# The clamp of phi's exponential moved from VectorE to GpSimd, in a kernel with a sliding-window and a linear attention block

## The chip, the cores and the metric

One core of a Trainium2 chip. The metric is the device time of one execution in microseconds (us). The kernel before was run three times: 291.31 us median, 289.54 to 292.64. Engine names as in the profile: PE is TensorE (PEld its weight loads), DVE is VectorE, ACT is ScalarE, POOL is GpSimd, SP is SyncE.

## What is computed

Two independent attention blocks, A and B, whose outputs stand side by side in the result. Each has an input x of 2048 tokens by 640, a weight wqkv of 640 by 1920 and wo of 640 by 640, in bf16, and 32 heads of 20. A is softmax attention over a window of 256 tokens. B is linear attention, and phi belongs to it:

```
phi = lambda t: jnp.where(t > 0, t + 1, jnp.exp(t)) + 1e-6
pq, pk = phi(q), phi(k)
kv = einsum("bhsd,bhse->bhde", pk, v);  z = einsum("bhsd->bhd", pk)
o = einsum("bhqd,bhde->bhqe", pq, kv) / (einsum("bhqd,bhd->bhq", pq, z)[..., None] + 1e-6)
```

The kernel writes phi(t) as max(t, 0) + min(exp(t) + 1e-6, 1 + 1e-6): for t > 0 the second part is the constant 1 + 1e-6, for t <= 0 the first part is 0. "The clamp" is the second part without the exponential (add, then minimum); "the sum" is the maximum with 0 and the addition.

## The kernel before

**Tiling.** Tokens are taken in 4 blocks (s = 0 to 3) of 512 (SB), and in tiles of 128. The 640 columns are 5 chunks of 128 (KT). A projection is a chain of 5 matmuls (L194) that accumulate in one PSUM bank, named "dense". There are three such banks (`dps`, 3 buffers); S_ps takes four banks, O_ps one.

**Two streams on PE.** The main stream is block A's attention, in 90 units. `scores` (L474) computes the scores of a unit into S_ps (L483), lets ACT make p from them with one exponential of 128x2048 (L491), and lets GpSimd cut p to the window with one or two selects (L505). `values` (L516) multiplies p with the values (L527) and, at the end of a group, normalises on DVE (L549, L550). `values` of a unit is issued after `scores` of the unit two later (LAG = 2). Into this stream a second one, `fill`, is woven: all projections, block B, and the output projections. After each unit `take` (L657) draws as many matmul columns from `fill` as the unit is due, an equal share.

**Queues.** The schedule is manual: each engine executes its instructions in the order in which the program issues them, and waits on semaphores for the other engines.

**phi.** `phi` (L200) is called at the end of a chain, with the bank as `src`. It issues the exponential on ACT at once (L203, into a tile e with 4 buffers). The clamp (L207) and the sum (L210) are put on the list `later`, and `flush` issues them: after the next cast that frees a bank (`evac`, L181), or after the exponential of the next phi, whichever is first. Both run on DVE. The sum is the last reader of the bank.

**Stages with phi.** Each of the eight stages calls phi five times, 40 in all:

- `b_kv(s)` (L355), four times: rows of k by the chains of `tok_rows`, in turn with the chains of the values (cast on DVE into vB), then the products of k and v (L377), added up in kv_acc and at last kv_bd (L385, L388). At the start GpSimd fills the ones in vB (L358); in `b_kv(3)` GpSimd cuts kv_bd to the own head with ten selects (L163).
- `b_q(s)` (L410), four times: phi of q. `b_q(0)` runs in turn with A's projections for block 3, `b_q(1)` alone, `b_q(2)` and `b_q(3)` in turn with output projections. `b_num` (L425) then reads phi of q (L436) and divides on DVE (L445 to L449).

In the order of time: b_kv(0) at about 41 to 61 us, b_kv(1) at 62 to 81, b_kv(2) at 81 to 100, b_kv(3) at 126 to 146, b_q(0) at 146 to 161, b_q(1) at 186 to 198, b_q(2) at 212 to 228, b_q(3) at 241 to 258.

**Other work in GpSimd's queue.** Three weight loads that it issues after the first unit's scores (L106, L617), the ones in vA (L309), and seven output DMAs of the output projections (L349), each of which waits for the last cast into its tile.

Of the kernel before, what the change touches and what calls it, by code (L numbers as in the profile page):

```python
# [10 lines left out]
ALU = mybir.AluOpType  # L11
# [41 lines left out]
def kernel(  # L53
# [10 lines left out]
    nc = tc.nc  # L64
# [10 lines left out]
    def pool(name, bufs, space=None):  # L75
        if space is None:
            return ctx.enter_context(tc.tile_pool(name=name, bufs=bufs))
        return ctx.enter_context(tc.tile_pool(name=name, bufs=bufs, space=space))
# [10 lines left out]
    op1 = pool("o1", 2)  # L89
# [86 lines left out]
    def flush():  # L176

        while later:
            later.pop(0)()
# [20 lines left out]
    def phi(dst, src, view=lambda t: t[:]):  # L200

        e = sp.tile([P, SB], BF16, name="e")
        nc.scalar.activation(out=view(e), in_=src, func=ACT.Exp)  # L203
        flush()

        def rest():
            nc.vector.tensor_scalar(  # L207
                out=e[:], in0=e[:], scalar1=1e-6, scalar2=1.0 + 1e-6, op0=ALU.add, op1=ALU.min
            )
            nc.vector.scalar_tensor_tensor(  # L210
                out=dst, in0=src, scalar=0.0, in1=view(e), op0=ALU.max, op1=ALU.add
            )

        later.append(rest)
# [140 lines left out]
    def b_kv(s):  # L355
# [4 lines left out]
        def done(tb, ps):  # L360
            if tb is None:
                phi(pk[:, :, SB:D], ps, lambda t: t[:].rearrange("p (t n) -> p t n", n=P))
            else:
                phi(pk[:, tb, 0:SB], ps[:])
# [45 lines left out]
    def b_q(s):  # L410
        xt = xB[NS + s]
        pq = pqp.tile([P, KT, SB], BF16, name="phi")
        pq_of[s] = pq
        for c in range(KT):
            ps = bank()
            yield from chain(
                ps[:],
                lambda kt: w_sb["B"][:, kt, c * P : (c + 1) * P],
                lambda kt: xt[:, kt, :],
                SB,  # L420
            )
            phi(pq[:, c, :], ps[:])
            yield End(SB)
# [292 lines left out]
```

## Time and profile before

| What | Value |
|---|---|
| Runs of the kernel before | 291.31 us median, 289.54 to 292.64 |
| The profiled execution | 290.37 us, span 288.5 us |
| Granted TensorE clock in it | 1.00 |
| L203, exponential of phi, ACT, 128x512 | 40 of 591 to 628 ns |
| L207, clamp, DVE, 128x512 bf16 | 40 of 282 to 1409 ns, median 373 |
| L210, sum, DVE, 128x512 | 40 of 691 to 694 ns |
| L491, exponential of the scores, ACT, 128x2048 | 90, mean 1878 ns |
| L505, selects of p, POOL | 178, 145.1 us; of 512 columns 120, mean 690 ns; of 1024 columns 56, mean 1114 ns |
| DMA, mean rate | 124 GB/s |

The profile is one execution on the chip. Busy time is the time in which an engine executes an instruction of the program. The chain is followed back from the last instruction: at each step to what released it, or to the instruction before it on its engine. In a line of a group, the numbers after the first bar are busy us and mean ns of one; after the second bar stand the idle time of the engine just before these instructions, and what ended it. In a line of the timeline, the first number is the start in us, the second the duration; xN means that N neighbours are merged, and in brackets stands the idle time before, and its releaser. "dense", "e", "p", "phi" are tiles of the kernel.

### The profile page before, as it was taken

How to read it: one execution, taken by the hardware profiler on the slowest of the kernel's cores; microseconds unless marked ns; L12 is line 12 of the kernel's file. 1: busy time of each engine (PE TensorE's matmuls, PEld its weight loads, DVE VectorE, ACT ScalarE, POOL GpSimd, SP SyncE). 2: the span in 40 equal slices, each digit the busy share in tenths (PEclk: the TensorE clock that was granted, in tenths of full speed). 3: DMA queues.
4: the chain of work that ended last, by engine and by line, in shares of the span. 5: the costliest groups of instructions: out<-in, count | busy, mean ns of one | idle time of the engine just before them, and what ended most of it. 6: DMA issues, size and time to landing. Idle time of an engine off the chain costs nothing.

```text
span 288.5 us, 8169 instructions
## 1 busy us (share of the span) xinstructions
PE 273.9 (95%) x3512; PEld 159.1 (55%) x3512; DVE 183.5 (64%) x409; ACT 193.4 (67%) x137; POOL 161.0 (56%) x212
## 2 busy tenths in 40 slices
PE   7999999999999999999999899998999999998995
PEld 7644555665666644565654554444545464545653
DVE  0666646847855744556657884458866887677861
ACT  2000058978889777789888767797688878976402
POOL 2000039657576666776699556666665766665620
PEclk9999999999999999999999999999999999999999
DMA  7997699999173172362062543079755145022486
GB/s 245 291 320 197 166 197 251 269 107 207 36 118 70 24 69 93 94 138 46 2 128 59 113 49 114 4 179 151 129 113 72 70 70 137 2 93 48 130 168 204
DMA packets 66676, 35.91 MB, mean 124 GB/s; under 512 B 50801, under 2 KB 65265, under 8 KB 66641
## 3 DMA queue, kind: packets, MB, share of 16 engines
q1 hardware_dynamic: 63792, 27.04, 49.5%
q0 software_dynamic: 1536, 7.05, 7.7%
q10 hardware_dynamic: 1312, 1.31, 1.4%
q8 instruction: 27, 0.44, 0.6%
q14 instruction: 9, 0.07, 0.1%
HBM read 12.45 MB, written 10.49 MB: 79 GB/s over the span
## 4 chain that ended last, share of the span: by engine, by line
PE 58%; ACT 17%; DVE 9%; issue 6%; DMA 6%; POOL 2%; SPq 0%; ACTq 0%; POOLq 0%
PE dense L194 35%; ACT p L491 14%; PE S_ps L483 10%; PE O_ps L527 9%; DMA k_scr<-st 2%; ACT e L203 2%; DMA kpad<-k_scr 2%; DVE phi L210 2%; PE dense L377 2%; DMA oT<-otokA 2%; PE dense L146 2%; DVE e L207 1%; POOL p L505 1%; DVE osb L185 1%; DVE otokB L449 1%
## 5 line engine op out<-in xcount | busy, mean ns | idle before, releaser
L491 ACT ACTIVATE p<-S_ps 128x2048 bf16<-128x2048 f32 x90 | 169.0, 1878 | 72.9 <-PE S_ps L483 68.2
L505 POOL TENSOR_SCALAR_AFFINE_SELECT p<-p 128x512 bf16<-128x512 bf16 (+2 forms) x178 | 145.1, 838 | 112.3 <-ACT p L491 112.2
L527 PEld LDWEIGHTS <-p 128*128 128x128 bf16 x1440 | 42.4, 96 | 19.7 <-issue 16.2
L527 PE MATMUL O_ps<-vA,p 128*128 128x21 bf16 x1440 | 51.1, 173 | 0.8 <-POOL p L505 0.7
L194 PE MATMUL dense<-wB,xB 128*128 128x320 bf16 (+2 forms) x320 | 49.3, 298 | 0.2 <-DVE phi L210 0.2
L194 PE MATMUL dense<-xA,wA 128*128 128x512 bf16 x200 | 46.1, 379 | 0.0
L185 DVE CAST st<-dense 128x512 bf16<-128x512 f32 x40 | 27.4, 690 | 20.5 <-PE dense L194 18.7
L483 PE MATMUL S_ps<-qpad,kpad 20*128 20x256 bf16 (+2 forms) x736 | 36.1, 269 | 2.9 <-ACT p L491 0.5
L185 DVE CAST osb<-dense 128x512 bf16<-128x512 f32 (+1 forms) x39 | 25.2, 647 | 16.1 <-PE dense L194 16.0
L194 PEld LDWEIGHTS <-xA 128*128 128x128 bf16 x320 | 26.4, 97 | 15.6 <-issue 1.5
L194 PEld LDWEIGHTS <-xB 128*128 128x128 bf16 x320 | 26.1, 97 | 13.3 <-issue 1.2
L483 PEld LDWEIGHTS <-kpad 20*128 20x128 bf16 x736 | 15.0, 92 | 32.4 <-issue 29.2
L194 PEld LDWEIGHTS <-wA 128*128 128x128 bf16 x200 | 18.5, 97 | 19.6
L210 DVE SCALAR_TENSOR_TENSOR phi<-dense,e 128x512 bf16<-128x512 f32 x40 | 27.7, 692 | 1.4
L194 PE MATMUL dense<-woA,oT 128*128 128x512 bf16 (+1 forms) x160 | 25.8, 299 | 2.7 <-DVE osb L185 1.6
L207 DVE TENSOR_SCALAR e<-e 128x512 bf16<-128x512 bf16 x40 | 21.2, 530 | 11.2 <-ACT e L203 11.1
L194 PE MATMUL dense<-xB,wB 128*128 128x512 bf16 x100 | 25.7, 378 | 0.9 <-DVE phi L210 0.8
L194 PE MATMUL dense<-wA,xA 128*128 128x320 bf16 x160 | 24.9, 299 | 1.4 <-DVE otokB L449 0.8
L194 PE MATMUL dense<-woB,xA 128*128 128x512 bf16 (+1 forms) x160 | 25.3, 299 | 0.5 <-PE dense L436 0.4
L203 ACT ACTIVATE e<-dense 128x512 bf16<-128x512 f32 x40 | 23.4, 593 | 0.2 <-PE dense L194 0.2
L185 DVE CAST vB<-dense 128x320 bf16<-128x320 f32 x32 | 15.2, 488 | 11.5 <-PE dense L194 11.1
L549 DVE RECIPROCAL recA<-O_ps 128x16 f32<-128x16 f32 (+1 forms) x34 | 8.5, 250 | 20.8 <-PE O_ps L527 20.7
(35 smaller groups left out, 152.0 us busy)
## 6 DMA issues: line engine op xcount, KB each, us to landing
out_dram<-osb POOLq DMA_DIRECT2D x7, 640.0 KB, 3.9
qpad<-q_scr SPq DMA_DIRECT2D x16, 160.0 KB
kpad<-k_scr SPq DMA_DIRECT2D x16, 160.0 KB
wA<-in_A_wqkv_dram SPq DMA_DIRECT2D x3, 800.0 KB
q_scr<-st SPq DMA_DIRECT2D x3, 640.0 KB
k_scr<-st SPq DMA_DIRECT2D x3, 640.0 KB
wB<-in_B_wqkv_dram SPq DMA_DIRECT2D x2, 800.0 KB
wB<-in_B_wqkv_dram POOLq DMA_DIRECT2D x1, 800.0 KB, 10.8
```

Of the source, the lines that this page charges most:

```text
L146: nc.tensor.matmul(ps[:, 0:P], lhsT=ident[:], rhs=ident[:], start=True, stop=True)
L185: nc.vector.tensor_copy(out=dst, in_=src)
L194: nc.tensor.matmul(dst, lhsT=lhs(kt), rhs=rhs(kt), start=(kt == 0), stop=(kt == KT - 1))
L203: nc.scalar.activation(out=view(e), in_=src, func=ACT.Exp)
L207: nc.vector.tensor_scalar(out=e[:], in0=e[:], scalar1=1e-6, scalar2=1.0 + 1e-6, op0=ALU.add, op1=ALU.min)
L210: nc.vector.scalar_tensor_tensor(out=dst, in0=src, scalar=0.0, in1=view(e), op0=ALU.max, op1=ALU.add)
L377: nc.tensor.matmul(pv, lhsT=pk[:, tb, c * P : (c + 1) * P], rhs=vB[:, tb, a : b + 1, :], start=(tb == 0), stop=(tb == TPS - 1),)
L483: nc.tensor.matmul(S_ps[:, j, blk * P : blk * P + n], lhsT=kt[32 * j : 32 * j + DH, g, ko : ko + P], rhs=q_pad[s][32 * j : 32 * j + DH, g, ...
L491: nc.scalar.activation(out=p[:], in_=S_ps[:], func=ACT.Exp, scale=scale)
L505: nc.gpsimd.affine_select(out=v, in_=v, pattern=[[0, 4], [0, b1 - b0], [sgn, P]], compare_op=ALU.is_ge, fill=0.0, base=0 if kind == "D" el ...
L527: nc.tensor.matmul(O_ps[:, slot, j, :], lhsT=p[:, j, b * P : (b + 1) * P], rhs=v_tok[kb // TPS][:, kb % TPS, 4 * gg + j, :], start=(first ...
L549: nc.vector.reciprocal(out=r[:, 0:n, :, :], in_=O_ps[:, :, :, DH:HV])
```

## The change

The clamp is issued on GpSimd instead of DVE, and at the call of phi, behind the exponential, instead of at the flush. Its operands are the same: e from SBUF to SBUF, in place. The sum stays on DVE and is issued at the flush as before.

```diff
         e = sp.tile([P, SB], BF16, name="e")
         nc.scalar.activation(out=view(e), in_=src, func=ACT.Exp)
+        nc.gpsimd.tensor_scalar(
+            out=e[:], in0=e[:], scalar1=1e-6, scalar2=1.0 + 1e-6, op0=ALU.add, op1=ALU.min
+        )
         flush()
 
         def rest():
-            nc.vector.tensor_scalar(
-                out=e[:], in0=e[:], scalar1=1e-6, scalar2=1.0 + 1e-6, op0=ALU.add, op1=ALU.min
-            )
             nc.vector.scalar_tensor_tensor(
                 out=dst, in0=src, scalar=0.0, in1=view(e), op0=ALU.max, op1=ALU.add
             )
```

## Prediction

> **What bounds the kernel now.** I read the page first: engines, chain, groups.
>
> ```profile
> span 288.5 us, 8169 instructions
> PE 273.9 (95%) x3512; PEld 159.1 (55%) x3512; DVE 183.5 (64%) x409; ACT 193.4 (67%) x137; POOL 161.0 (56%) x212
> ...
> PE 58%; ACT 17%; DVE 9%; issue 6%; DMA 6%; POOL 2%; SPq 0%; ACTq 0%; POOLq 0%
> ...
> L505 POOL TENSOR_SCALAR_AFFINE_SELECT p<-p 128x512 bf16<-128x512 bf16 (+2 forms) x178 | 145.1, 838 | 112.3 <-ACT p L491 112.2
> ...
> L210 DVE SCALAR_TENSOR_TENSOR phi<-dense,e 128x512 bf16<-128x512 f32 x40 | 27.7, 692 | 1.4
> ...
> L207 DVE TENSOR_SCALAR e<-e 128x512 bf16<-128x512 bf16 x40 | 21.2, 530 | 11.2 <-ACT e L203 11.1
> ...
> L203 ACT ACTIVATE e<-dense 128x512 bf16<-128x512 f32 x40 | 23.4, 593 | 0.2 <-PE dense L194 0.2
> ```
>
> PE (TensorE) is the engine without air: busy 95%, 58% of the chain. DVE (VectorE) has 36% idle, so its 21.2 us of clamps (L207) are not in themselves on the path. DVE's 9% of the chain is places where PE waits for it to give back a "dense" PSUM bank; there are three. POOL (GpSimd) idles while it waits for ACT's next p.
>
> I then read the busy time in stretches of time. From 40 us on, PE is idle 9.6 us in all (sum of the gaps in its timeline): that is the most any cure of waits there can bring. Last, I read the timeline of the stage b_q(1) engine by engine, here POOL and then DVE:
>
> ```profile
> 189.16 1.36 POOL L505 TENSOR_SCALAR_AFFINE_SELECT p<-p 128x512 bf16<-128x512 bf16 x2 [0.72 <-ACT p L491]
> 191.91 1.78 POOL L505 TENSOR_SCALAR_AFFINE_SELECT p<-p 128x1024 bf16<-128x1024 bf16 x2 [1.39 <-ACT p L491]
> 194.37 1.78 POOL L505 TENSOR_SCALAR_AFFINE_SELECT p<-p 128x512 bf16<-128x512 bf16 x2 [0.68 <-ACT p L491]
> ```
> ```profile
> 189.61 0.37 DVE L207 TENSOR_SCALAR e<-e 128x512 bf16<-128x512 bf16 x1 [1.21 <-ACT e L203]
> 190.02 0.69 DVE L210 SCALAR_TENSOR_TENSOR phi<-dense,e 128x512 bf16<-128x512 f32 x1
> 190.63 0.28 DVE L207 TENSOR_SCALAR e<-e 128x512 bf16<-128x512 bf16 x1
> 190.94 0.69 DVE L210 SCALAR_TENSOR_TENSOR phi<-dense,e 128x512 bf16<-128x512 f32 x1
> 192.36 0.79 DVE L207 TENSOR_SCALAR e<-e 128x512 bf16<-128x512 bf16 x1 [0.73 <-ACT e L203]
> 193.19 0.69 DVE L210 SCALAR_TENSOR_TENSOR phi<-dense,e 128x512 bf16<-128x512 f32 x1
> 194.82 0.37 DVE L207 TENSOR_SCALAR e<-e 128x512 bf16<-128x512 bf16 x1 [0.94 <-ACT e L203]
> 195.22 0.69 DVE L210 SCALAR_TENSOR_TENSOR phi<-dense,e 128x512 bf16<-128x512 f32 x1
> ```
>
> The reader is to see the order. ACT runs an e right behind a p (the exponential of the scores). When p ends, POOL starts that p's selects, 1.36 to 2.0 us long. So when e is ready, POOL has just begun them, while DVE is often waiting for e. The clamp then runs beside the selects and the sum (L210) starts about 0.5 us before they end.
>
> **What leaves DVE.** 40 clamps, 21.2 us. Fifteen of them take 282 to 284 ns, all with POOL idle or nearly so; the rest 371 to 1409 ns beside selects. 40 x 0.283 = 11.3 us is work, 9.9 us is waiting. I count no gain for it directly: the sum that follows a clamp now waits for POOL instead, and DVE's spare 36% covers the rest. POOL's selects lose the same disturbance (minimum 668 ns, mean 690 for the 512 form); POOL waits 112 us for ACT, so that is nothing too.
>
> **What POOL gets.** 40 clamps of 128x512 bf16 to bf16, not shown in this trace. Nearest POOL row: the select of the same shape and types, 668 to 690 ns; the memset of 128 columns takes 670. I take c = 0.68 us. Below, DVE's undisturbed 0.28 is the bound; above, twice the select, 1.36. The Trainium skill (GPSIMD Engine Reference, 4.1 Engine selection) sends elementwise work to VectorE and puts GpSimd at about 2x the time with two inputs, roughly line rate with one. Read as twice DVE's 0.283 that would be 0.57, an estimate, and the sum below 305.2 instead of 306.9; no run here shows the operation yet. Load: POOL's 161.0 us become 188, still below PE's. Per p (2.46 us apart) it has 145.1/90 = 1.6 us of selects; one clamp fits.
>
> **Where the clamp stands in POOL's queue.** It is issued where phi is called, that is after the selects of the p that precedes e on ACT, and before those of the next. So its start is the end of those selects, not the end of e. Behind it on POOL wait the next selects and the output DMAs (L349). Two units lie between a select and the matmuls that read it: the selects of 66.21 to 67.69 are read at 68.99, so 1.3 us are spare and one clamp is covered; two in one unit take it up. Behind the waiting sum on DVE stand casts that free the other banks and the A normalisation (L549, L550).
>
> **What PE notices.** For each of the 40 sums I took from the timeline the time between its end and the first matmul into the bank that it frees (three or four chains later, in program order). The least distance in the kernel is 0.05 us: PE was waiting. Thirteen of the 40 have 0.05 to 0.08, three have 0.2 to 0.3, the others 0.65 to 2.4. For a sum with no slack the new stall is about 0.5 (selects still running) + 0.68 + 0.04 (semaphore) = 1.22. A stall moves all later work, so a sum whose p and e were already under way gets it forgiven; one whose p is moved pays again.
>
> b_q(1), worked through. First sum: selects end 190.52, clamp 191.20, sum 191.24 to 191.93; its bank was taken at 190.76, now 191.98: **+1.22**. Third: selects 191.91 to 193.69, unmoved; clamp to 194.37, sum to 195.10; its matmul was at 193.93, moved already to 195.15: +0. Fourth: p is moved by 1.22, selects end 197.37, clamp 198.05, sum to 198.78, matmul 198.83 against 195.97 + 1.22: **+1.64**. Second and fifth have 1.2 and 1.05 to spare. Together 2.9.
>
> The other stages in the same way. b_kv(0): POOL is busy with weight DMA issues, selects and a memset until 47.26; first clamp to 47.94, sum to 48.67, bank wanted at 47.69: +1.0; selects of the next two units then slip, second sum ends at 52.54 instead of 50.30: 2.25 in all; the fourth (slack 0.69) and fifth add 0.6 each: 3.4. b_kv(1): 0.35 (slack 0.23, d = 0.54), then 1.2: 1.55. b_kv(2) and b_kv(3): in the first four of five, slack covers the delay; the last (slack 0.05 at 97.78 and 142.90) costs 1.2 each. b_q(0): POOL runs eight kv_bd selects (L163) before the selects of p, which end at 152.65; first clamp 153.33, sum 3.4 later, slack 2.36; memset to 154.0, selects to 155.8, second clamp to 156.5, sum to 157.2 instead of 154.13, no slack: 3.1; the fourth adds 1.2: 4.3. b_q(2): 0.5 (selects end 220.04, sum was at 220.24), 1.2, 0.25: 1.9. b_q(3): slacks 1.04 to 2.24 cover all: 0.
>
> Sum: 3.4 + 1.55 + 1.2 + 1.2 + 4.3 + 2.9 + 1.9 + 0 = 16.5 us. On the profiled execution (290.37 us: span 288.5 and 1.9 around it) that gives 306.9. The median of the runs is 0.9 above that execution, within their spread. I say **307**. In these sums c counts some 15 times: c = 0.28 gives 301, c = 1.36 gives 317.
>
> **Rivals.**
> 1. Faster: the waiting between DVE and POOL is what costs, and it ends. L207's 9.9 us of waiting and its 21.2 us fall away from DVE, banks are cast sooner. The decisive point is whether the clamp finds POOL free when e is ready; then the sum starts no later. For it: for 14 of the 40 POOL is through 0.2 us or more before the sum began (251.19 against 251.99). Against it: in 12 of the 13 without slack the selects are still running. PE's idle time in the eight stretches with phi is 6.2 us; if half goes, 287. Beside this: the Trainium skill (SBUF — State Buffer, Who interferes with whom) says that a two-port VectorE operation and a GpSimd operation lock each other out for a whole instruction. The 282 against 371 to 1409 ns agree.
> 2. No change: the stalls fall in places where ACT's loop of S_ps and p (0.4 + 1.88 + 0.2 = 2.46 us a unit) would have held PE anyway, and PE regains them. Against it: PE waits for ACT's p at S_ps 0.5 us in all, so hardly anything is there to regain from. 290 to 293.
> 3. Far slower: a POOL clamp takes two selects' time or more. Then 1.6 + 1.4 us per unit exceed 2.46, selects fall behind and the values matmuls (L527, now waiting 3.5 us for POOL) wait as well: 15 x 0.7 more, 317, and up from there.
>
> **Chances.** Forecast 0.80, rival 1 0.08, rival 2 0.07, rival 3 0.05. The range 297 to 317 takes in both bounds of c and some 4 us of stalls that are regained. Measurement tells about 1% from no change; faster 0.08, same 0.07, slower 0.85.
>
> **What would show it.** L207 on POOL, about 680 ns each; L210 with idle time before it, released by POOL, of some 20 to 30 us; PE's wait for phi L210 up from 0.9 to over 10 us and PE idle after 40 us from 9.6 to some 25; DVE busy 162. Most of it at 47 to 58, 150 to 160 and 190 to 199 of the old time, nothing at 244 to 258. It is wrong if L210 follows its e as closely as before, if c is under 0.4 or over 1, or if PE waits for O_ps instead of banks.

## The result, and the profile after

The changed kernel takes 354.94 us (median of 4 runs, 349.22 to 357.72) against 291.07 us of the kernel before in the same series: ratio 1.207, 95% interval 1.196 to 1.219. Executions of one kernel fall into two states, the slower one with a lower granted clock; medians here are over all executions, ratios over the faster state alone on both sides. Forecast were 307 us and a range of 297 to 317. The direction was right, the size was not: the loss is four times the 16 us forecast. The profiled execution took 353.49 us, span 351.8, mean granted TensorE clock 0.922 (1.00 before).

The page after: span, engines, chain, and the groups that answer to those of before. L204 is the clamp in its new place.

```profile
span 351.8 us, 8166 instructions
PE 297.0 (84%) x3512; PEld 165.4 (47%) x3512; DVE 163.4 (46%) x369; ACT 194.0 (55%) x137; POOL 236.8 (67%) x252
...
POOL 38%; PE 37%; ACT 11%; DMA 5%; DVE 5%; issue 3%; SPq 0%; ACTq 0%; POOLq 0%
PE dense L194 23%; POOL p L505 18%; POOL e L204 18%; ACT p L491 11%; PE S_ps L483 6%; PE O_ps L527 4%; DVE phi L210 2%; DMA k_scr<-st 2%; DMA kpad<-k_scr 2%; PE dense L146 1%; DMA oT<-otokA 1%; PE dense L377 1%; PE dense L436 1%; POOL kv_bd L163 1%; DVE otokB L449 1%
...
L505 POOL TENSOR_SCALAR_AFFINE_SELECT p<-p 128x512 bf16<-128x512 bf16 (+2 forms) x178 | 143.2, 828 | 94.9 <-ACT p L491 92.8
L204 POOL TENSOR_SCALAR e<-e 128x512 bf16<-128x512 bf16 x40 | 76.8, 1919 | 3.4
L210 DVE SCALAR_TENSOR_TENSOR phi<-dense,e 128x512 bf16<-128x512 f32 x40 | 27.7, 692 | 105.1 <-POOL e L204 105.1
```

Three things are to be seen. A clamp on POOL takes 1919 ns, not 680. POOL, 2% of the chain before, is now its largest part: selects 18%, clamps 18%. And the sum (L210), which hardly waited before (1.4 us), stands idle 105 us for POOL's clamps, with all that is queued behind it on DVE.

POOL's timeline in the stage b_q(1), which is now at 230 to 248 us:

```profile
232.08 1.32 POOL L505 TENSOR_SCALAR_AFFINE_SELECT p<-p 128x512 bf16<-128x512 bf16 x2 [0.72 <-ACT p L491]
233.48 3.92 POOL L204 TENSOR_SCALAR e<-e 128x512 bf16<-128x512 bf16 x2
237.47 1.73 POOL L505 TENSOR_SCALAR_AFFINE_SELECT p<-p 128x1024 bf16<-128x1024 bf16 x2
239.29 1.92 POOL L204 TENSOR_SCALAR e<-e 128x512 bf16<-128x512 bf16 x1
```

DVE at the same time, then the first matmul that waited for DVE on PE:

```profile
235.44 0.69 DVE L210 SCALAR_TENSOR_TENSOR phi<-dense,e 128x512 bf16<-128x512 f32 x1 [4.11 <-POOL e L204]
237.43 0.69 DVE L210 SCALAR_TENSOR_TENSOR phi<-dense,e 128x512 bf16<-128x512 f32 x1 [1.31 <-POOL e L204]
241.24 0.69 DVE L210 SCALAR_TENSOR_TENSOR phi<-dense,e 128x512 bf16<-128x512 f32 x1 [3.12 <-POOL e L204]
```
```profile
236.18 1.86 PE L194 MATMUL dense<-xB,wB 128*128 128x512 bf16 x4 [2.45 <-DVE phi L210]
```

The order is the one that the prediction named: selects, clamp, sum, bank, matmul. But from 232.08 on POOL has no gap of more than 0.1 us left in this stretch. Its next selects wait for the clamps instead of for ACT. PE's waits for the sum over the whole span (us in total, times, longest), before:

```profile
PE dense L194 <- DVE phi L210: 0.9, 3, 0.5
```

and after:

```profile
PE dense L194 <- DVE phi L210: 34.5, 23, 3.4
PE dense L436 <- DVE phi L210: 7.4, 6, 1.6
```

Where the time is, by stage (from the first score matmul of one unit to that of another; us):

| Stage | Before | After | More | Forecast | POOL busy after |
|---|---|---|---|---|---|
| b_kv(0) | 23.4 | 34.1 | 10.7 | 3.4 | 26.9 |
| b_kv(1) | 20.0 | 26.9 | 7.0 | 1.55 | 21.6 |
| b_kv(2) | 17.9 | 24.7 | 6.8 | 1.2 | 22.8 |
| b_kv(3) | 17.5 | 25.0 | 7.5 | 1.2 | 22.7 |
| b_q(0) | 16.3 | 25.9 | 9.5 | 4.3 | 22.0 |
| b_q(1) | 11.3 | 18.2 | 6.9 | 2.9 | 16.9 |
| b_q(2) | 16.1 | 22.6 | 6.5 | 1.9 | 21.2 |
| b_q(3) | 15.8 | 19.4 | 3.6 | 0 | 17.9 |
| the stretches between, without phi | 92.4 | 96.9 | 4.5 | 0 | 58.4 |

All but 4.5 of the 63 us lie in the stages with phi. POOL is busy 79 to 94% of each of them.

### The profile page after: what moved, and what is told of

It reads as the page before. It is cut to its first block, busy times and chain, and to the rows that moved or that the text cites. A ratio compares the mean times of both kernels' runs of the same rounds, so it can differ in the third digit from the quotient of the medians.

```text
span 351.8 us, 8166 instructions
## 1 busy us (share of the span) xinstructions
PE 297.0 (84%) x3512; PEld 165.4 (47%) x3512; DVE 163.4 (46%) x369; ACT 194.0 (55%) x137; POOL 236.8 (67%) x252
## 3 DMA queue, kind: packets, MB, share of 16 engines
q10 hardware_dynamic: 1312, 1.31, 1.1%
## 4 chain that ended last, share of the span: by engine, by line
POOL 38%; PE 37%; ACT 11%; DMA 5%; DVE 5%; issue 3%; SPq 0%; ACTq 0%; POOLq 0%
PE dense L194 23%; POOL p L505 18%; POOL e L204 18%; ACT p L491 11%; PE S_ps L483 6%; PE O_ps L527 4%; DVE phi L210 2%; DMA k_scr<-st 2%; DMA kpad<-k_scr 2%; PE dense L146 1%; DMA oT<-otokA 1%; PE dense L377 1%; PE dense L436 1%; POOL kv_bd L163 1%; DVE otokB L449 1%
## 5 line engine op out<-in xcount | busy, mean ns | idle before, releaser
L505 POOL TENSOR_SCALAR_AFFINE_SELECT p<-p 128x512 bf16<-128x512 bf16 (+2 forms) x178 | 143.2, 828 | 94.9 <-ACT p L491 92.8
L204 POOL TENSOR_SCALAR e<-e 128x512 bf16<-128x512 bf16 x40 | 76.8, 1919 | 3.4
L210 DVE SCALAR_TENSOR_TENSOR phi<-dense,e 128x512 bf16<-128x512 f32 x40 | 27.7, 692 | 105.1 <-POOL e L204 105.1
L194 PE MATMUL dense<-wB,xB 128*128 128x320 bf16 (+2 forms) x320 | 56.7, 319 | 23.3 <-DVE phi L210 22.8
L527 PEld LDWEIGHTS <-p 128*128 128x128 bf16 x1440 | 42.8, 97 | 21.6 <-issue 16.9
L194 PEld LDWEIGHTS <-xB 128*128 128x128 bf16 x320 | 27.5, 102 | 40.7 <-issue 28.2
L194 PE MATMUL dense<-xB,wB 128*128 128x512 bf16 x100 | 32.6, 459 | 10.0 <-DVE phi L210 10.0
L483 PE MATMUL S_ps<-qpad,kpad 20*128 20x256 bf16 (+2 forms) x736 | 38.5, 286 | 2.3 <-ACT p L491 0.5
L194 PEld LDWEIGHTS <-xA 128*128 128x128 bf16 x320 | 26.9, 99 | 17.0 <-issue 3.3
L483 PEld LDWEIGHTS <-kpad 20*128 20x128 bf16 x736 | 13.9, 94 | 36.8 <-issue 34.3
L194 PE MATMUL dense<-woA,oT 128*128 128x512 bf16 (+1 forms) x160 | 27.0, 307 | 3.6 <-DVE otokB L449 2.0
L194 PE MATMUL dense<-wA,xA 128*128 128x320 bf16 x160 | 25.9, 307 | 2.0 <-DVE phi L210 1.3
L194 PEld LDWEIGHTS <-wB 128*128 128x128 bf16 x100 | 9.9, 109 | 20.9 <-issue 16.3
L185 DVE CAST vA<-dense 128x320 bf16<-128x320 f32 x32 | 15.6, 492 | 9.0 <-PE dense L194 9.0
```

The costliest lines, as they stand in the source:

```text
L185: nc.vector.tensor_copy(out=dst, in_=src)
L194: nc.tensor.matmul(dst, lhsT=lhs(kt), rhs=rhs(kt), start=(kt == 0), stop=(kt == KT - 1))
L204: nc.gpsimd.tensor_scalar(out=e[:], in0=e[:], scalar1=1e-6, scalar2=1.0 + 1e-6, op0=ALU.add, op1=ALU.min)
L210: nc.vector.scalar_tensor_tensor(out=dst, in0=src, scalar=0.0, in1=view(e), op0=ALU.max, op1=ALU.add)
L483: nc.tensor.matmul(S_ps[:, j, blk * P : blk * P + n], lhsT=kt[32 * j : 32 * j + DH, g, ko : ko + P], rhs=q_pad[s][32 * j : 32 * j + DH, g, ...
L505: nc.gpsimd.affine_select(out=v, in_=v, pattern=[[0, 4], [0, b1 - b0], [sgn, P]], compare_op=ALU.is_ge, fill=0.0, base=0 if kind == "D" el ...
```

## Experiments

Theory 1: the order was seen rightly, and only the price of the clamp on POOL was wrong. It has two forms: the loss comes by way of late banks (1a), or POOL is overfull (1b). The rivals: the earlier place of the clamp, the wait on DVE as such, or the lower clock is what costs.

**The clamp's price by itself (e1).** Behind the last instruction of the kernel before, POOL runs a series on SBUF tiles filled with ones, three of each; `ts` issues three tensor_scalar instructions in place:

```diff
+        kw = dict(scalar1=1e-6, scalar2=1.0 + 1e-6, op0=ALU.add, op1=ALU.min)
...
+        for n in (SB, 128, 256, 1024):
+            ts(a[:, 0:n], **kw)
+        ts(f, **kw)
+        ts(a[:, 0:SB], scalar1=1.0, scalar2=None, op0=ALU.min)
+        ts(a[:, 0:SB], scalar1=1e-6, scalar2=None, op0=ALU.add)
+        ts(a[:, 0:SB], scalar1=1e-6, scalar2=1.0, op0=ALU.add, op1=ALU.mult)
...
```

> The kernel before, with a series of GpSimd instructions of 128 partitions behind its last one, three of each; their durations are the result, the total time is not compared. Theory A (the clamp is slow by the element): add-and-minimum of 512 columns 1.92 us, 128 columns about 0.55, 256 about 1.0, 1024 about 3.8. Theory B (a fixed price per instruction): 128 columns still about 1.5. If it is the second operation that costs, minimum alone or add alone takes about half of 1.92; if it is the minimum, add-and-multiply is as short as the select. Select of 512 columns: 0.68 in every theory.

Groups of POOL's instructions in this run, by shape (L696 is the clamp in four widths and on f32, L707 a multiplication of two tiles, L705 a copy, L711 the select):

```profile
L696 POOL TENSOR_SCALAR osb<-osb 128x1024 bf16<-128x1024 bf16 x3 | 10.9, 3626 | 0.2
L696 POOL TENSOR_SCALAR kv_acc<-kv_acc 128x512 f32<-128x512 f32 x3 | 5.8, 1919 | 0.2
...
L707 POOL TENSOR_TENSOR osb<-osb 128x512 bf16<-128x512 bf16 x3 | 3.5, 1151 | 0.2
L696 POOL TENSOR_SCALAR osb<-osb 128x256 bf16<-128x256 bf16 x3 | 3.2, 1066 | 0.2
...
L696 POOL TENSOR_SCALAR osb<-osb 128x128 bf16<-128x128 bf16 x3 | 1.9, 639 | 0.2
L711 POOL TENSOR_SCALAR_AFFINE_SELECT osb<-osb 128x512 bf16<-128x512 bf16 x3 | 1.8, 615 | 0.2
L705 POOL COPY osb<-osb 128x512 bf16<-128x512 bf16 x3 | 1.8, 613 | 0.2
```

The same groups in short windows, which part the instructions of 512 columns: first the clamp, then add alone, then add and multiply:

```profile
L696 POOL TENSOR_SCALAR osb<-osb 128x512 bf16<-128x512 bf16 x3 | 5.8, 1922 | 0.3
```
```profile
L696 POOL TENSOR_SCALAR osb<-osb 128x512 bf16<-128x512 bf16 x3 | 4.5, 1491 | 0.2
```
```profile
L696 POOL TENSOR_SCALAR osb<-osb 128x512 bf16<-128x512 bf16 x3 | 1.9, 619 | 0.2
```

Theory A holds. From 256 to 1024 columns the clamp costs (3626 - 1066) / 768 = 3.33 ns per column. The second operation is not half the price: add alone, and minimum alone (1485 to 1497), take 1.49 us. Add and multiply together take 0.62 us, as short as the select and the copy. So at one shape and with the same bytes the operations in the instruction set the price on POOL, by a factor of three, and bf16 is no cheaper than f32. DVE did the same clamp in 0.283 us undisturbed, 6.8 times faster.

**The prediction's own price (e2).**

```diff
-        nc.gpsimd.tensor_scalar(
-            out=e[:], in0=e[:], scalar1=1e-6, scalar2=1.0 + 1e-6, op0=ALU.add, op1=ALU.min
+        nc.gpsimd.affine_select(
+            out=e[:], in_=e[:], pattern=[[0, SB]], compare_op=ALU.is_ge,
+            fill=0.0, base=1, channel_multiplier=0,
         )
```

> The changed kernel with the clamp's computation left out: in its place in GpSimd's queue stands a select of the same 128x512 tile that keeps every element (about 0.68 us). Theory 1 (the order select, clamp, sum, bank was seen rightly and only the price of the clamp was wrong): the prediction's own sum, 307 us, 302 to 312, and the same stages carry it. Rival (the early issue, or DVE's wait for GpSimd as such, costs, whatever the price): over 325. Rival (nothing is lost when the clamp is short): under 296.

305.29 us, ratio 1.045 (1.034 to 1.057). The select took 612 ns (median). Theory 1 stands, and by stages: 2.8, 1.6, 1.1, 1.1, 3.8, 2.4, 1.9 and 0.0 us more than before, against 3.4, 1.55, 1.2, 1.2, 4.3, 2.9, 1.9 and 0 in the prediction. PE's waits in this run, longest in total first (us in total, times, longest):

```profile
PE dense L194 <- DVE phi L211: 9.9, 10, 1.9
PE dense L437 <- DVE phi L211: 2.4, 3, 1.3
```

It is the bank that the sum gives back, as forecast (L211 and L437 are L210 and L436 of the kernel before).

**Place without engine (e3), engine without place (e6).** In e3 the clamp goes back to DVE but keeps its early place; in e6 it is on GpSimd at its old place, in `rest` (first edit against the changed kernel, second against the kernel before).

```diff
-        nc.gpsimd.tensor_scalar(
+        nc.vector.tensor_scalar(
```
```diff
         def rest():
-            nc.vector.tensor_scalar(
+            nc.gpsimd.tensor_scalar(
                 out=e[:], in0=e[:], scalar1=1e-6, scalar2=1.0 + 1e-6, op0=ALU.add, op1=ALU.min
             )
```

> The clamp back on DVE, but issued at the call of phi, before the flush, where the change put it on GpSimd. Theory 1: the place alone does little, 288 to 296 us. Rival (the place in the order is what costs): over 310.

> The clamp on GpSimd, but issued at the flush, where it stood before the change: the engine alone is changed, not the place. Theory 1 (the price on GpSimd is what costs): 345 to 365 us, as the change. Rival (the early place costs a good part, as it did on DVE, where it cost 14 us): under 340.

e3: 305.72 us, ratio 1.043 (1.031 to 1.055). I had expected nothing: a miss. By its profile (an execution of 310.07 us) the early place is bad on DVE because the clamp of one phi now stands ahead of the flush that gives back the bank of the phi before, and waits for its exponential (42.5 us in all, 35 times); PE's waits for the sum grew from 0.9 to 8.6 us. No run tests this reading by itself. e6: 376.64 us, ratio 1.294 (1.287 to 1.301), also outside what I expected. On GpSimd the early place is the better one, by some 22 us: at the flush the clamp stands behind still more selects (on average 2.8 start between the exponential and its clamp, against 2.0 in the change, and the clamp starts 3.6 us behind the exponential's end, against 2.4), and the sum waited 126.9 us against 105.1. So the place in a queue counts on both engines, in opposite directions; in the change the early place limits the damage.

**Late banks or a full POOL (e4, e9).** DVE takes max(t, 0) from the bank into phi's place, and adds the clamped e in SBUF two phi later, so that the bank does not wait for POOL. In e4 the maximum stands behind the exponential, in e9 ahead of it:

```diff
+        nc.vector.tensor_scalar(
+            out=dst, in0=src, scalar1=0.0, scalar2=None, op0=ALU.max
+        )
         nc.scalar.activation(out=view(e), in_=src, func=ACT.Exp)
...
-            nc.vector.scalar_tensor_tensor(
-                out=dst, in0=src, scalar=0.0, in1=view(e), op0=ALU.max, op1=ALU.add
-            )
+            nc.vector.tensor_tensor(out=dst, in0=view(e), in1=dst, op=ALU.add)
-        later.append(rest)
+        adds.append(rest)
+        flush_adds(2)
...
```

> The changed kernel, clamp on GpSimd, but the bank no longer waits for it: DVE takes max(t, 0) from the bank at once, and the addition of the clamped e is done in SBUF two phi later. The 1e-6 stays in the clamp. Theory 1a (banks given back late are the whole loss): 290 to 300 us. Theory 1b (GpSimd itself is overfull in the stages of phi: per stage 1.6 us of selects per unit and 5 x 1.92 of clamps are more than the stage's time before, in sum some 34 us): 315 to 330. Rival (GpSimd's lock on VectorE or anything that grows with the clamps themselves): no better than 350.

> As e4, but DVE's maximum is issued before the exponential: in e4 it waited for the exponential (47 us in all), since two engines that read one bank are put in order, so that e4 did not free the banks at once. Now the bank is free when the exponential is through, and the addition of the clamped e follows two phi later; the clamp stays on GpSimd. Theory 1a (late banks are the loss): 290 to 305 us. Theory 1b (GpSimd is overfull with clamps of 1.92 us between the selects; p comes late for the values matmuls): 325 to 350, with PE waiting for GpSimd's selects for tens of us.

e4: 345.12 us, ratio 1.182 (1.173 to 1.191). That lies between the ranges that I had given, and it did not test what it should, since DVE's maximum waited for the exponential. e9 does: 345.75 us, ratio 1.189 (1.180 to 1.198). Theory 1a falls, and the time is in the range of 1b. POOL's timeline in e9, in b_kv(3):

```profile
149.95 1.73 POOL L515 TENSOR_SCALAR_AFFINE_SELECT p<-p 128x512 bf16<-128x512 bf16 x2
151.77 1.97 POOL L213 TENSOR_SCALAR e<-e 128x512 bf16<-128x512 bf16 x1
153.81 1.49 POOL L515 TENSOR_SCALAR_AFFINE_SELECT p<-p 128x512 bf16<-128x512 bf16 x2
155.38 1.92 POOL L213 TENSOR_SCALAR e<-e 128x512 bf16<-128x512 bf16 x1
```

One pair of selects and one clamp take 3.6 to 3.9 us, and there is one such pair per unit, where a unit took 2.46 us before. The 34 us named for 1b in e4 spread the clamps over whole stages. In the kernel before, the five phi of a stage stand within 3 to 5 units, 36 units in all, so 1.1 clamps fall on each. By the selects' 1.6 us and the clamp's 1.92, POOL is short of (1.6 + 1.1 x 1.92 - 2.46) x 36 = 45 us there, an estimate. With the banks free, PE meets the same POOL elsewhere. The list of its waits in e9:

```profile
PE O_ps L537 <- POOL p L515: 14.7, 27, 1.7
PE dense L446 <- DVE phi L219: 14.7, 10, 3.8
```

The first is the values matmuls waiting for p (0.5 us in the change), with 23.9 us more at their weight loads (4.1). The second is the end of a stage, where phi's last additions wait for their clamps. Freeing the banks in this form gains 9 us of the 63 by the medians (354.9 against 345.8), 5 by the ratios, whose intervals overlap. That is what is left after a price of the form itself: e12 below has nearly the same form without GpSimd and takes 301.7 us, 10 more than the kernel before. So late banks may be worth up to some 20 us. The rest changes its place and stays: e9 and e12 differ by 44 us, near the 45 estimated.

**No clamp (e5).** The clamp is left out on both engines (the new instruction is deleted).

> The clamp is left out of the computation, on both engines; the sum on DVE waits for the exponential alone. It bounds what any engine could give that takes the clamp off DVE at no price. Theory 1: PE's whole idle time after 40 us was 9.6 us before, of which DVE's clamp is a part: 283 to 289 us. Rival (DVE's clamps were a hidden bound, the lock's 9.9 us of waiting were on the path): under 282.

289.37 us, ratio 0.992 (0.987 to 0.997), just above the range given. This is the most that taking the clamp off DVE could have given in this order, at no price at all: 0.8%. PE's idle time after 40 us stayed at 9.6 us. The lock's 9.9 us of waiting on DVE, the ground of the first rival, was hardly on the path.

**Two prices between (e10, e11).** Minimum alone on GpSimd (1.49 us; the 1e-6 is left out), and the clamp of half the columns (1.07 us; the other half is left out):

```diff
-            out=e[:], in0=e[:], scalar1=1e-6, scalar2=1.0 + 1e-6, op0=ALU.add, op1=ALU.min
+            out=e[:], in0=e[:], scalar1=1.0, scalar2=None, op0=ALU.min
```
```diff
-            out=e[:], in0=e[:], scalar1=1e-6, scalar2=1.0 + 1e-6, op0=ALU.add, op1=ALU.min
+            out=e[:, 0 : 2 * P], in0=e[:, 0 : 2 * P], scalar1=1e-6, scalar2=1.0 + 1e-6, op0=ALU.add, op1=ALU.min
```

> The changed kernel with minimum(e, 1) alone on GpSimd, 1.49 us for 512 columns by e1; the 1e-6 is left out. Prediction's sum with the price put right (16.5 us at 0.68, 15 per us more): 290 + 16.5 + 12 = 319. With an overfull GpSimd on top (1.6 + 1.1 x 1.49 = 3.2 us per unit against 2.46): 325 to 340.

> The changed kernel with only 256 of the 512 columns clamped, on GpSimd, 1.07 us by e1; the clamp of the other half is left out. Prediction's sum: 290 + 16.5 + 6 = 312. GpSimd per unit 1.6 + 1.1 x 1.07 = 2.8 us against 2.46, a little overfull: 312 to 322. If the loss simply grows with the clamp's time from zero (63 us for 1.92): 325.

333.04 us (ratio 1.139, 1.127 to 1.151) and 323.65 us (median of 4, 319.04 to 325.27). In order of the clamp's time: 0.61 us 305, 1.07 us 324, 1.49 us 333, 1.92 us 355. From the first to the last that is 50 us for 1.31 us (47 by the ratios), 36 to 38 us per us: on average as if nearly every one of the 40 clamps counted in full, though the three steps are uneven (18, 9 and 22 us). The prediction's sum had 15. e10 fits a full POOL; e11 lies a little above what I gave for that and below the 325 of plain proportion, within its spread of both, and tells nothing apart.

**The clock (e7).** Twelve matmuls of 128x128 more per unit in the stages with phi, into an unused part of the O_ps bank:

```diff
...
+            if n == len(todo) // 2 and unit in PHI:
+                for _ in range(12):
+                    nc.tensor.matmul(
+                        spare, lhsT=ident[:], rhs=ident[:],
+                        start=False, stop=False, skip_group_check=True,
+                    )
...
```

> The changed kernel with 12 matmuls of 128x128 more per unit in the stages with phi, into an unused part of the O_ps bank, so that PE has fewer gaps (0.7 us of work a unit where it stood idle 0.8 to 1.5). It tests whether the lower granted clock (0.92) is a cause of its own: PE was busy 23 us longer than before the change. Theory 2a (the slower matmuls are on the path): the granted clock rises to 0.97 or more and the time falls by 10 us or more, under 344. Theory 2b (GpSimd's queue is the bound in these stages and hides the slower clock): the clock rises and the time stays within 350 to 362.

350.29 us, ratio 1.205 (1.198 to 1.213): the same as the change within the intervals, while the granted clock rose from 0.92 to 0.98. The filler is itself 44.0 us of work, so that PE was busy 313.9 us, 17 more than in the change; the run does not price the clock alone. It shows that in these stages PE had time for more work and for slower work, so the 23 us by which PE was busy longer in the change (297.0 against 273.9) are in the main an effect and not a cause. In the change the granted clock fell to 0.50 eleven times, 54.6 us in all, behind or in waits of 1.2 to 3.4 us; in e7 13.7 us in all, before never. The Trainium skill (TensorE: Matmul & The Clock Gate, HAM oscillation) says that idle gaps of more than some 3.4 us bring the half clock back. The trace agrees in the direction, with 0.76 to 0.98 granted in the stages where PE waited for POOL and 1.00 before, but only one of its waits reached 3.4 us. A small part is a cause: in three stretches without phi the clock was 0.95, 0.96 and 0.88 in the change, which took 2.2 us more than before; in e7 it was 1.00 there, and they took no more than before.

**A form without GpSimd (e8, e12).** DVE takes max(t, 0) + 1e-6 from the bank first and adds min(e, 1) later, in one instruction from SBUF; behind the exponential in e8, ahead of it in e12:

```diff
+        nc.vector.tensor_scalar(
+            out=dst, in0=src, scalar1=0.0, scalar2=1e-6, op0=ALU.max, op1=ALU.add
+        )
...
             nc.vector.scalar_tensor_tensor(
-                out=dst, in0=src, scalar=0.0, in1=view(e), op0=ALU.max, op1=ALU.add
+                out=dst, in0=view(e), scalar=1.0, in1=dst, op0=ALU.min, op1=ALU.add
             )
```

> A form meant to be better than both: DVE takes max(t, 0) + 1e-6 from the bank at once into phi's place, and later adds min(e, 1) to it in SBUF with one instruction. GpSimd has no part in phi. The bank is free when the exponential and the first DVE instruction have read it. If the late return of banks is what is left of PE's waits: 283 to 289 us. If the added DVE work (two of some 0.65 us instead of 0.53 and 0.69) and its waits eat that up: 290 to 296.

> As e8 (all of phi on DVE and ACT), with DVE's maximum issued before the exponential, so that it does not wait for it; the bank is free after the exponential. If what is left of PE's waits is late banks: 284 to 289 us. If the exponential now waits for DVE, or the sum with two SBUF inputs waits for GpSimd's selects (677 to 1477 ns in e8) and holds DVE: 290 to 300.

301.68 us (ratio 1.038, 1.034 to 1.041) and 301.69 us (1.034, 1.026 to 1.043). Both are slower than the kernel before, and above every range that I had given. In e8 DVE's maximum waited 33.9 us for the exponential. In e12 that is gone, but the exponential waits for DVE (10.5 us), and PE's scores for ACT's p (8.6 us against 0.5): the wait moved into ACT's loop. No version here that computes phi whole beats the kernel before.

## Why the prediction was wrong

**The step that failed is the price:** "Nearest POOL row: the select of the same shape and types, 668 to 690 ns; ... I take c = 0.68 us. Below, DVE's undisturbed 0.28 is the bound; above, twice the select, 1.36." The clamp took 1.92 us (e1, and L204 in the change). Shape and types were the nearest that the trace had, but e1 shows that at one shape the operation sets the price on POOL. Twice the select was no bound: the trace of before held not one arithmetic instruction on POOL, and nothing in it could exclude three times. The range should have reached as far as rival 3.

**The second step follows from it:** "In these sums c counts some 15 times." That holds as long as POOL has gaps in which the clamp fits, and the trace of before says how long: 2.46 us per unit less 1.6 of selects, both in the prediction, with 40 clamps on 36 units, leaves 0.8 us for each. Above that every clamp counts. With the right price the old sum gives 16.5 + 15 x 1.24 = 35 us; measured are 63. Taken together, from e2's 305.3 us on, 0.2 us more at 15 us per us and 1.1 us more at 40 give 352 us, an estimate, against 354.9 measured.

**Right was the way that it goes, for a short instruction.** e2 is the test: with 0.61 us in the same place, 305.3 us against the forecast of 307, stage by stage within 0.7 us. Selects first, then the clamp, then the sum, then the bank; stalls forgiven where p and e were under way.

**The signs that it named:** DVE busy 163.4 (forecast 162). L210 idle 105 us and released by POOL (forecast 20 to 30; 50.9 in e2, so this was sized too low at the right price too). PE waiting 34.5 + 7.4 us for phi (over 10). PE idle after the first scores 50.1 (some 25; 21.6 in e2). "Most of it" in b_kv(0), b_q(0) and b_q(1) failed: 27 of the 63 us (9.0 of 14.7 in e2), since every stage paid when POOL was full. "Nothing at 244 to 258" failed: b_q(3) lost 3.6 us, since slacks of 1.0 to 2.2 us cover a clamp of 0.68 and not one of 1.92 (in e2 it lost 0.0). The sign "if c is ... over 1" for a wrong prediction came true.

**Two readings were off, without weight here.** "DVE's 9% of the chain" is 26 us, but PE's waits for DVE at "dense" banks were 5.5 us in all before. And of the fifteen short clamps (282 to 284 ns) two, at 197.12 and 245.12, ran wholly beside selects.

**The rivals.** The first, faster by the end of the lock, is bounded by e5: 0.8%. Nor did a lock slow DVE down in the change: it was busy 163.4 us, against 162.3 before without its clamps. The second, no change because PE regains the stalls, has nothing for it: e2 lost what the sum said. The third, a POOL clamp of two selects' time or more with selects falling behind, is what happened. It had 0.05, and "317 and up from there" was the right side without a size. The Trainium skill (GPSIMD Engine Reference, 4.1 Engine selection) names the doubling for two inputs and roughly line rate for one; the clamp has one. Even the doubling, read as 0.57 us, is off by more than three times here: 1.92 measured against 0.283 is a factor of 6.8. Its advice to leave plain elementwise work on VectorE held.

**Open.** Why the pair add and multiply is three times as fast on POOL as the pair add and minimum was not tried further; other pairs were not timed. How the 63 us divide between late banks and late p is not a fixed split: in e9 PE waits for p and for phi's last additions in place of the banks, and e9 bounds the part of the banks only roughly.

## What to carry to other kernels

Before work moves to an engine that has not done this operation in the trace, take its price as unknown by several times, not as that of the instruction of the same shape; three copies behind the kernel's last instruction measured it here. Then compare price times count with the gaps of that engine in the stages where the work falls, not over the span: POOL was 56% busy over the span, and yet had room for only 0.8 us per clamp. And ask first what the move could give at best: leaving the clamp out altogether was worth 0.8%.

## Not expected of the hardware

- GpSimd's tensor_scalar of 128x512 takes 1.92 us for add and minimum, 1.49 for add or minimum alone, 0.62 for add and multiply; a select and a copy take 0.61, a product of two tiles 1.15. bf16 and f32 clamps alike take 1.92.
- DVE's addition of two SBUF tiles (128x512 bf16) took 414 to 1233 ns beside POOL's work (e9), its sum with one operand in PSUM 691 to 693 ns in the change, whatever POOL did. In the change POOL's selects of 512 columns had a mean of 680 ns, against 690 with the clamp on DVE.
- The granted clock fell to 0.50 behind short waits of PE too, and while PE was busy again: in the change from 287.0 to 290.4 us, when PE had no gap, after waits of 1.2 and 1.6 us that ended at 280.6 and 284.4.
